# Two PSUM copies moved to ScalarE, the decay exp written into zeroed tiles, and the whole instruction order planned anew, in a fused RWKV-6 and squared-ReLU kernel

## The chip, the cores and the metric

The kernel runs on one core of a Trainium2 chip. The time is that of one whole execution in device microseconds (us). The profile of an execution has a *span*, from its first to its last instruction; the time is about 2 us longer. The *ramp* is the first 36 us, in which TensorE still waits for loads and for the other engines; behind it TensorE is saturated, which means that it has work all the time.

## The reference

```python
def _attn_ref(r, k, v, w, u):                 # (4, 8, 768, 48) each, u (8, 48)
    for t in range(S):
        cur = np.einsum('bhd,bhe->bhde', u[None] * kt, vt)
        y[:, :, t] = np.einsum('bhd,bhde->bhe', rt, state + cur)
        state = wt[:, :, :, None] * state + np.einsum('bhd,bhe->bhde', kt, vt)

def _moe_ref(x, w_in, w_out):                 # x (3072, 384), w_in (384, 2048)
    r = np.maximum(x @ w_in, 0.0)
    return (r * r) @ w_out
```

The kernel cuts the sequence into 24 chunks of 128 steps, 6 for each of 4 batch rows. In a chunk the recurrence becomes matmuls: cumulative sums of log w, decayed r and k, scores, and a state that is handed on. Two finished chunks make one of 12 blocks of the feed-forward part.

## The kernel before

Every operation is a small function, and a long list of words calls them. Each engine runs its own part of the list in order. A word in the wrong place makes an engine stand behind a wait although later work is ready.

```python
ps_cp = pool("ps_cp", bufs=1, PSUM)       # two banks: cumulative sum, its exp, scores, in turn
ps_tr_pool = pool("ps_tr", bufs=1, PSUM)  # one bank: transposes, state update, transposed y, in turn
# (pools abridged)

    other_head = consts.tile([C, HP, 2], BF16)
    nc.gpsimd.memset(other_head[:], 0.0)
    nc.gpsimd.memset(other_head[0:DP, :, 1:2], -30000.0)
    nc.gpsimd.memset(other_head[DP:C, :, 0:1], -30000.0)

    def q_(s):                                   # row sums of r*u*k
        nc.vector.reduce_sum(q[:], tiles.pop(("qp", s))[:], axis=AX.X)

    def ac_(s):                                  # decay of the state over the chunk
        a_c = tiles["a_c", s] = a_small.tile([C, HP, 2], FP32, name="a_c")
        nc.scalar.activation(a_c[:], tiles["su", s][:, DM:DM + 2 * HP]..., AF.Exp)

    def rkt_(s):                                 # transposed r and k out of PSUM
        rkT = tiles["rkT", s] = a_mid.tile([C, 2, HP, C], BF16, name="rkT")
        nc.vector.tensor_copy(rkT[:], tiles.pop(("tr", s))[:])

    def su_(s):                                  # state update
        for p in range(HP):
            nc.tensor.matmul(ps_su[:, p * 2 * D:(p + 1) * 2 * D], rdec[:, 1, 2 * p:2 * p + 2, :],
                             v_bf[:, 2 * p:2 * p + 2, :], start=True, stop=True)
        nc.tensor.matmul(ps_su[:, DM:DM + 2 * HP], ident[:], other_head[:], start=True,
                         stop=False, skip_group_check=True)
        for p in range(HP):
            nc.tensor.matmul(ps_su[:, DM + 2 * p:DM + 2 * p + 2], lw[:, 2 * p:2 * p + 2, :],
                             ones2[:], start=False, stop=True, skip_group_check=True)
    # ... (cut: all other functions)
    order = """
        ld:0:w ld:0:k warm:6:0 ld:0:u ld:0:r ld:1:w lw:0 ld:0:v cum:0 ld:1:r ub exp:0 ld:1:k ...
    """                                          # 1052 words, cut
```

`warm:n:b` is n filler matmuls on a zero tile, `ld` a load, `ld:4:I` the fifth slab of w_in (a slab is an eighth of a weight matrix; it is cast to bf16 before it is used). A tile of two heads has 128 rows; a state block is valid only where head meets head, and the mask matmul of -30000 makes exp give zero elsewhere.

Of the kernel before, what the change touches and what calls it, by code (L numbers as in the profile page):

```python
# [8 lines left out]
FP32 = mybir.dt.float32  # L9
FP16 = mybir.dt.float16  # L10
BF16 = mybir.dt.bfloat16
AF = mybir.ActivationFunctionType
# [4 lines left out]
def kernel(  # L17
# [11 lines left out]
    nc = tc.nc  # L29
# [3 lines left out]
    C = 128  # L33
    DP = 64
    HP = H // 2
    NCH = S // C
    DM = H * D
# [10 lines left out]
    consts = ctx.enter_context(tc.tile_pool(name="consts", bufs=1))  # L48
# [81 lines left out]
    ident = consts.tile([C, C], BF16)  # L130
# [6 lines left out]
    other_head = consts.tile([C, HP, 2], BF16)  # L137
    nc.gpsimd.memset(other_head[:], 0.0)
    nc.gpsimd.memset(other_head[0:DP, :, 1:2], -30000.0)
    nc.gpsimd.memset(other_head[DP:C, :, 0:1], -30000.0)  # L140
# [64 lines left out]
    def ac_(s):  # L205
        a_c = tiles["a_c", s] = a_small.tile([C, HP, 2], FP32, name="a_c")
        nc.scalar.activation(a_c[:], tiles["su", s][:, DM:DM + 2 * HP].rearrange("p (a e) -> p a e", e=2), AF.Exp)
# [14 lines left out]
    def rkt_(s):  # L222
        rkT = tiles["rkT", s] = a_mid.tile([C, 2, HP, C], BF16, name="rkT")
        nc.vector.tensor_copy(rkT[:], tiles.pop(("tr", s))[:])  # L224
# [30 lines left out]
    def su_(s):  # L255
        rdec, v_bf, lw = tiles["rdec", s], tiles["v", s], tiles["lw", s]
        ps_su = tiles["su", s] = ps_tr_pool.tile([C, 512], FP32, name="tr")
        for p in range(HP):
            nc.tensor.matmul(ps_su[:, p * 2 * D:(p + 1) * 2 * D], rdec[:, 1, 2 * p:2 * p + 2, :],  # L259
                             v_bf[:, 2 * p:2 * p + 2, :], start=True, stop=True)  # L260
        nc.tensor.matmul(ps_su[:, DM:DM + 2 * HP], ident[:], other_head[:], start=True,
                         stop=False, skip_group_check=True)
        for p in range(HP):
            nc.tensor.matmul(ps_su[:, DM + 2 * p:DM + 2 * p + 2], lw[:, 2 * p:2 * p + 2, :],  # L264
                             ones2[:], start=False, stop=True, skip_group_check=True)
# [103 lines left out]
    def ld_(n, x):  # L369
# [7 lines left out]
        ld:0:w ld:0:k warm:6:0 ld:0:u ld:0:r ld:1:w lw:0 ld:0:v cum:0 ld:1:r ub exp:0 ld:1:k warm:2:1 rd:0 lw:1 ld:2:w  # L377
        tr:0 uc cum:1 rkt:0 ld:1:v v:0 ku:0 warm:1:2 exp:1 su:0 ld:2:k warm:8:3 ac:0 rd:1 ku:1 ld:2:r lw:2 ts:0 ld:0:I
        qp:1 p:0 tr:1 pm:0 v:1 ld:2:v qp:0 warm:3:0 rkt:1 ld:3:w cum:2 sn:0 warm:1:1 exp:2 q:1 su:1 ku:2 warm:6:2 ld:3:r
        ac:1 rd:2 vq:1 ld:3:k q:0 p:1 warm:2:3 ts:1 vq:0 ld:1:I pm:1 tr:2 qp:2 y:0 lw:3 ld:4:w warm:2:0 v:2 rkt:2 cum:3  # L380
        ld:5:w warm:3:1 exp:3 ysb:0 ku:3 q:2 yt:0 y:1 ld:3:v xt:0 rd:3 warm:1:2 sn:1 su:2 ld:2:I ac:2 ysb:1 p:2
        cast:i:0:0 qp:3 warm:2:3 ts:2 ld:4:k pm:2 yt:1 vq:2 warm:2:0 xt:1 ld:3:I lw:4 tr:3 ld:4:v sn:2 q:3 m1:0:0:1 lw:5
        rkt:3 vq:3 v:3 y:2 rl:0:0 p:3 cast:i:0:1 ld:4:r su:3 pm:3 cast:i:1:0 m1:0:1:2 ku:4 ld:5:k rl:0:1 m1:0:2:3 ysb:2
        ac:3 cum:4 rw:5 ts:3 ld:5:r y:3 exp:4 cast:i:1:1 yt:2 warm:1:0 sn:3 ld:4:I ysb:3 m1:0:3:1 xt:2 v:4 yt:3 rd:4
        qp:4 ld:5:I warm:3:2 xt:3 ld:6:I rl:0:2 ld:7:I ku:5 cum:5 q:4 tr:4 ld:0:O rl:0:3 ld:1:O m1:1:0:0 gt:0:0 exp:5
        ld:2:O m1:1:2:2 kw:5 ld:3:O rkt:4 ld:5:v m1:1:3:3 rl:1:2 gt:0:1 su:4 qp:5 cast:i:2:0 m1:1:1:1 rd:5 ac:4 m1:1:4:2
        vq:4 rl:1:3 ts:4 p:4 rl:1:0 cast:i:2:1 m1:0:4:3 sn:4 rl:1:1 pm:4 ld:4:O tr:5 cast:i:3:0 ld:5:O m1:1:5:0 gt:1:1
        ld:6:w rl:0:4 m1:0:6:1 gt:1:0 rl:1:4 y:4 m1:0:5:3 rl:1:5 rkt:5 m1:1:6:2 cast:i:3:1 rl:0:5 ysb:4 rl:0:6 m1:0:7:0
        cast:o:0:1 cast:o:0:0 m1:1:7:3 gt:1:2 p:5 rl:0:7 m2:1:1:0:1 ld:6:O gt:0:2 cast:o:1:0 ld:7:O yt:4 cast:o:1:1
        m2:0:0:0:0 ld:7:w rl:1:6 q:5 m2:1:1:1:1 v:5 pm:5 vq:5 m2:0:1:0:2 cast:o:2:0 m2:0:1:1:2 ld:6:k rl:1:7 y:5  # L390
        cast:o:2:1 m2:0:0:1:0 xt:4 ysb:5 ld:6:r m2:0:0:2:0 lw:6 gt:1:3 rw:6 yt:5 cum:6 m2:1:1:2:1 xt:5 gt:0:3 cast:o:3:0
        m2:0:1:2:2 ld:7:r m1:2:0:3 exp:6 cast:o:3:1 ld:7:k m2:1:1:3:1 lw:7 m2:0:1:3:2 ku:6 rl:2:0 ld:6:v m2:0:0:3:0
        os:1:1 ld:8:w kw:6 m1:2:4:3 os:0:0 m2:1:0:0:1 ld:7:v rw:7 qp:6 rd:6 rl:2:4 m2:1:0:1:1 ld:8:k ku:7 os:0:1 q:6
        cum:7 tr:6 exp:7 ld:9:w m1:2:1:0 kw:7 rkt:6 m1:2:2:3 lw:8 ld:10:w qp:7 rd:7 m1:2:6:2 v:6 ld:9:k rl:2:2 vq:6 q:7
        tr:7 rw:8 p:6 ld:11:w rkt:7 rl:2:1 ku:8 m1:2:5:3 v:7 pm:6 ld:10:k su:6 kw:8 rl:2:5 m1:2:3:0 ld:8:r lw:10
        m2:1:0:2:1 gt:2:0 ac:6 rl:2:3 y:6 ts:6 ld:9:r p:7 lw:9 m2:1:0:3:1 sn:6 pm:7 rl:2:6 ld:8:v m2:2:1:0:3 vq:7 os:1:0
        m1:2:7:0 ysb:6 ld:11:k cum:8 gt:2:1 yt:6 y:7 exp:8 ld:10:r qp:8 m2:2:0:0:2 ysb:7 m2:2:1:1:3 ld:12:w xt:6 ku:9
        rd:8 rw:9 yt:7 m2:2:0:1:2 store:1:1 xt:7 gt:2:2 ld:9:v cum:9 kw:9 rl:2:7 tr:8 q:8 ld:12:k m1:3:2:1 exp:9 rkt:8
        vq:8 m1:3:3:0 ld:10:v rl:3:2 rd:9 qp:9 m2:2:0:2:2 v:8 m1:3:4:1 gt:2:3 rl:3:3 ld:13:w ku:10 tr:9 rl:3:4 m1:3:0:0
        ld:11:v rkt:9 rw:10 m1:3:5:1 rl:3:0 gt:3:1 ld:13:k su:7 kw:10 m2:2:0:3:2 ac:7 ld:14:k rl:3:5 ts:7 m1:3:1:0  # L400
        os:2:0 gt:3:2 ld:11:r su:8 sn:7 rl:3:1 p:8:1:2 q:9 v:10 m1:3:6:0 store:0:1 gt:3:0 lw:12 ld:12:r vq:9 m2:2:1:2:3
        pm:8 ac:8 ld:13:r rl:3:6 m2:2:1:3:3 ku:11 v:9 store:1:0 ts:8 m2:3:0:0:0 os:2:1 ld:12:v qp:10 pmh:9:0 y:8 lw:11
        m1:3:7:3 pmh:9:1 rw:12 sn:8 ld:14:r su:9 v:11 ysb:8 cum:10 m2:3:0:1:0 qp:11 ac:9 store:2:1 rl:3:7 ts:9 ld:14:w
        y:9 exp:10 q:10 yt:8 ku:12 m2:3:0:2:0 ysb:9 ld:13:v m2:3:1:0:1 xt:8 rd:10 sn:9 rw:11 yt:9 ld:15:r m2:3:1:1:1
        xt:9 q:11 kw:12 cum:12 lw:13 tr:10 exp:12 qp:12 m1:4:2:2 ld:16:r rkt:10 m1:4:0:3 gt:3:3 rl:4:2 ld:15:w su:10
        kw:11 rd:12 m1:4:3:2 ac:10 rl:4:0 store:0:0 m2:3:1:2:1 ku:13 ld:16:w ts:10 rl:4:3 cum:11 ld:14:v m1:4:4:3 gt:4:1
        exp:11 vq:10 m2:3:0:3:0 q:12 ld:15:v rl:4:4 m1:4:5:2 rd:11 qp:13 lw:14 m1:4:1:3 os:3:0 ld:15:k sn:10 q:13 tr:11
        rl:4:1 m2:3:1:3:1 rkt:11 ld:16:v rl:4:5 m1:4:6:0 gt:4:0 os:3:1 p:10:3:2 rl:4:6 store:3:1 gt:4:2 ld:16:k m1:4:7:1
        rw:14 pm:10 ld:17:w tr:12 rw:13 store:3:0 m2:4:0:0:0 kw:13 ld:17:v pmh:11:0 y:10 cum:13 pmh:11:1 vq:11
        m2:4:1:0:3 v:13 ysb:10 rl:4:7 m2:4:0:1:0 ku:14 ld:18:v rkt:12 lw:15 ld:17:r y:11 exp:13 m2:4:1:1:3 qp:14 ysb:11  # L410
        yt:10 m2:4:0:2:0 gt:4:3 xt:10 ld:17:k vq:12 m2:4:1:2:3 v:12 rd:13 ld:18:k rw:15 yt:11 kw:14 m2:4:1:3:3 xt:11
        q:14 ld:19:v cum:14 su:12 ku:16 m1:5:2:2 ac:12 exp:14 ts:12 ld:18:w m2:4:0:3:0 ku:15 tr:13 os:4:1 rd:14 m1:5:4:1
        qp:15 os:4:0 rl:5:2 rkt:13 m1:5:0:3 kw:15 rl:5:4 q:15 p:12:0:2 rl:5:0 sn:12 su:13 pm:12 m1:5:3:1 ac:13 v:14
        ku:17 m1:5:1:3 rl:5:3 ts:13 y:12 rl:5:1 cum:15 vq:14 pmh:13:0 tr:14 lw:16 m1:5:5:1 ysb:12 vq:13 lw:17 m1:5:6:3
        rkt:14 exp:15 sn:13 ld:20:v pmh:13:1 yt:12 ld:19:k m1:5:7:0 store:4:1 xt:12 gt:5:0 y:13 store:2:0 rl:5:5 su:14
        gt:5:1 ld:21:v m2:5:1:0:2 ac:14 ld:20:k v:15 ts:14 m2:5:0:0:1 rl:5:6 ysb:13 ld:19:w m2:5:1:1:2 rw:16 rd:15 yt:13
        kw:16 m2:5:0:1:1 xt:13 cum:16 rl:5:7 gt:5:2 tr:15 ld:18:r qp:16 m1:6:2:3 exp:16 rkt:15 m1:6:0:0 ld:20:w qp:17
        rl:6:2 rd:16 m2:5:1:2:2 rl:6:0 store:4:0 sn:14 su:15 q:16 m2:5:0:2:1 ac:15 v:16 gt:5:3 p:14:3:0 vq:15 lw:18
        ts:15 m2:5:0:3:1 rw:18 pm:14 sn:15 rw:17 m2:5:1:3:2 lw:19 tr:16 kw:17 pmh:15:0 os:5:1 y:14 os:5:0 cum:17
        pmh:15:1 m1:6:1:2 ku:18 v:17 store:5:0 ysb:14 m1:6:4:3 ld:19:r exp:17 kw:18 rkt:16 ld:21:w y:15 ld:22:w m1:6:3:1  # L420
        rl:6:4 rd:17 qp:18 yt:14 rl:6:1 m1:6:6:0 ysb:15 ku:19 xt:14 ld:21:k m1:6:7:3 rl:6:3 yt:15 gt:6:0 cum:18 ld:20:r
        m1:6:5:2 xt:15 vq:16 rl:6:6 m1:7:2:1 ld:21:r gt:6:1 rl:6:5 m1:7:0:0 q:17 rl:6:7 ld:22:r m1:7:3:2 gt:6:2 exp:18
# [59 lines left out]
```

## Time and profile before

| | before |
|---|---|
| time, four executions on one chip | 191.76 to 191.83, median 191.81 |
| the profiled execution: time, span | 192.89, 191.1 |
| busy: TensorE, VectorE, ScalarE, GpSimd | 97, 74, 70, 59 per cent |

The row PE of the page gives busy tenths of TensorE in 40 slices, and the row DMA the same of the 16 DMA engines. The chain follows what ended last back to what released it. The lines stand in the prediction.

### The profile page before, as it was taken

What the parts mean: (1) busy time and instruction counts of PE and PEld (TensorE: products, weight loads), DVE (VectorE), ACT (ScalarE), POOL (GpSimd) and SP (SyncE); (2) the same over time, 40 slices, a digit from 0 to 9 for tenths busy, and PEclk for the clock granted to TensorE, in tenths of its full rate; (3) what the DMA queues carried; (4) which work ended last, traced back from release to release, by engine and by line L of the source; (5) the groups of instructions that cost most, each with busy time, mean ns of one, the idle gap of its engine ahead of it and who ended that gap; (6) DMA issues with size and microseconds to landing.
All of it is one profiled execution on the core that took longest, in us unless ns stands there. A gap on an engine that the chain in (4) does not pass through costs nothing.

```text
span 191.1 us, 4952 instructions
## 1 busy us (share of the span) xinstructions
PE 184.7 (97%) x1955; PEld 137.1 (72%) x1958; DVE 140.5 (74%) x211; ACT 132.9 (70%) x284; POOL 113.2 (59%) x128
## 2 busy tenths in 40 slices
PE   6999999899999999999999999999999999999993
PEld 2444578676687787777788778777698778676873
DVE  3349999797378978799688999888787787463220
ACT  3533687887887978789589798858598468524640
POOL 7294959400985989984995897579297713000000
PEclk9999999999999999999999999999999999999998
DMA  6999999998998979999798939940620000003313
GB/s 120 204 244 244 230 215 307 372 314 229 208 196 173 234 150 234 226 219 221 171 202 171 230 105 192 192 81 3 139 71 0 0 3 0 5 0 141 110 41 124
DMA packets 107817, 30.20 MB, mean 158 GB/s; under 512 B 100498, under 2 KB 106771, under 8 KB 107795
## 3 DMA queue, kind: packets, MB, share of 16 engines
q1 hardware_dynamic: 107794, 29.89, 67.6%
q8 instruction: 15, 0.25, 0.6%
q14 instruction: 8, 0.06, 0.1%
HBM read 25.17 MB, written 4.72 MB: 156 GB/s over the span
## 4 chain that ended last, share of the span: by engine, by line
PE 80%; SPq 13%; DMA 3%; issue 1%; ACT 0%; DVE 0%
PE mm L340 32%; PE mm L316 31%; SPq L67 11%; PE tr L220 5%; DMA w_st<-in_moe_w_in_dram 3%; PE y L285 2%; PE cp L238 2%; PE tr L301 2%; PE cp L194 2%; SPq L90 2%; PE y L290 2%; PE tr L259 1%; PE mm L355 1%; PE mm L238 1%; PE tr L264 1%
## 5 line engine op out<-in xcount | busy, mean ns | idle before, releaser
L316 PE MATMUL mm<-xT,wi_sb 128*128 128x256 bf16 x576 | 72.4, 273 | 1.1 <-ACT wi_sb L105 0.8
L340 PE MATMUL mm<-wo_sb,gt 128*128 128x384 bf16 x368 | 69.2, 326 | 0.0
L325 ACT ACTIVATE rl<-mm 128x512 f16<-128x512 f32 x96 | 55.6, 599 | 14.0 <-PE mm L316 12.2
L316 PEld LDWEIGHTS <-wi_sb 128*128 128x128 bf16 x576 | 54.1, 98 | 9.7 <-ACT wi_sb L105 1.1
L340 PEld LDWEIGHTS <-gt 128*128 128x128 bf16 x368 | 34.1, 98 | 17.6
L333 DVE TENSOR_TENSOR gt<-rl 128x1024 bf16<-128x1024 f16 x48 | 36.7, 780 | 9.1 <-ACT rl L325 9.0
L176 POOL TENSOR_TENSOR ku<-rk_raw,u_bc 128x384 f32<-128x384 f32 x24 | 25.7, 1074 | 9.0 <-DMA rk_raw<-in_k_dram 5.9
L168 POOL TENSOR_TENSOR rk_raw<-rk_raw,rw 128x384 f32<-128x384 f32 x19 | 20.9, 1099 | 16.4 <-ACT rw L164 13.2
L188 POOL TENSOR_TENSOR vq<-v_raw,q 128x384 f32<-128x384 f32 x24 | 22.1, 920 | 13.9 <-DVE q L184 10.1
L211 DVE TENSOR_TENSOR rdec_buf<-rk_raw,cp 128x768 bf16<-128x768 f32 x24 | 22.8, 950 | 8.0 <-ACT cp L201 4.4
L180 POOL TENSOR_TENSOR qprod<-rk_raw,ku 128x384 f32<-128x384 f32 x24 | 25.8, 1079 | 1.6 <-issue 1.1
L224 DVE COPY rkT<-tr 128x1024 bf16<-128x1024 bf16 x24 | 16.5, 688 | 10.0 <-PE tr L220 10.0
L277 POOL TENSOR_TENSOR S<-t_state,a_c 128x384 bf16<-128x384 f32 x20 | 18.0, 900 | 7.8 <-DVE t_state L273 5.3
L243 DVE TENSOR_TENSOR pmT<-cp,tri_strict 128x1024 bf16<-128x1024 f32 x16 | 19.5, 1219 | 3.0 <-PE cp L238 3.0
L345 ACT ACTIVATE o_sb<-mm 128x384 f32<-128x384 f32 x23 | 11.1, 492 | 9.9 <-PE mm L340 9.9
L295 DVE TENSOR_TENSOR y_sb<-vq,y 128x384 bf16<-128x384 f32 x24 | 13.2, 549 | 6.1 <-PE y L290 4.3
L304 ACT COPY xT<-tr 128x384 bf16<-128x384 bf16 x24 | 11.5, 481 | 7.3 <-PE tr L301 7.1
L367 PE MATMUL mm<-warm 128*128 128x512 bf16 x40 | 14.2, 474 | 1.4 <-DVE warm L133 1.3
L220 PE MATMUL tr<-ident,rdec_buf 128*128 128x128 bf16 x192 | 15.1, 223 | 0.1
L220 PEld LDWEIGHTS <-rdec_buf 128*128 128x128 bf16 x192 | 12.9, 100 | 3.1 <-issue 1.0
L160 ACT ACTIVATE lw_buf<-w_raw 128x384 bf16<-128x384 f32 x24 | 12.3, 522 | 3.1 <-POOL lw_buf L146 1.8
L184 DVE TENSOR_REDUCE q<-qprod 128x8 f32<-128x384 f32 x24 | 13.1, 545 | 0.1
(59 smaller groups left out, 197.2 us busy)
## 6 DMA issues: line engine op xcount, KB each, us to landing
w_raw<-in_w_dram SPq DMA_DIRECT2D x24, 192.0 KB, 3.8
rk_raw<-in_k_dram SPq DMA_DIRECT2D x24, 192.0 KB, 3.9
rk_raw<-in_r_dram SPq DMA_DIRECT2D x24, 192.0 KB, 3.7
v_raw<-in_v_dram SPq DMA_DIRECT2D x24, 192.0 KB, 4.0
out_dram<-o_sb SPq DMA_DIRECT2D x23, 192.0 KB, 3.1
w_st<-in_moe_w_in_dram SPq DMA_DIRECT2D x8, 384.0 KB, 5.7
w_st<-in_moe_w_out_dram SPq DMA_DIRECT2D x8, 384.0 KB, 7.1
out_dram<-o_sb SPq DMA_DIRECT2D x2, 96.0 KB, 1.6
```

The source lines that it names most:

```text
L67: nc.sync.dma_start(out=dst, in_=src[b, :, c * C:(c + 1) * C, :].rearrange("h c d -> c h d"))
L168: nc.gpsimd.tensor_mul(k_s, k_s, tiles.pop(("rw", s))[:])
L176: nc.gpsimd.tensor_mul(ku[:], raw["rk", s][:, 1], u_bc[:])
L180: nc.gpsimd.tensor_mul(qp[:], raw["rk", s][:, 0], tiles.pop(("ku", s))[:])
L188: nc.gpsimd.tensor_mul(vq[:], raw["v", s][:], tiles.pop(("q", s))[:, :, None].to_broadcast([C, H, D]))
L211: nc.vector.tensor_mul(rdec[:, :, :, 0:D], raw["rk", s][:], tiles.pop(("cs", s))[:, :, 0:DM].rearrange("p a (h d) -> p a h d", h=H))
L220: nc.tensor.transpose(ps_tr[:, i, p, :], rdec[:, i, 2 * p:2 * p + 2, :], ident[:])
L243: nc.vector.tensor_mul(pmT[:].rearrange("p e a t -> p (e a) t"), tiles.pop(("p", s))[:].rearrange("p e (a t) -> p (e a) t", a=HP), tri_str ...
L316: nc.tensor.matmul(ps1[:, j * width:(j + 1) * width], wi_sb[:, kk, n * 128:(n + 1) * 128], xT[:, kk, s0 * C:s0 * C + width], start=(kk == ...
L325: nc.scalar.activation(tiles["rl", i, q][:, j], tiles.pop(("m1", i, g))[:], AF.Relu, scale=RS)
L333: nc.vector.tensor_mul(tiles["gt", i][:, 4 * q:4 * q + 4, :].rearrange("p a b -> p (a b)"), rl, rl)
L340: nc.tensor.matmul(tiles["m2", i, mt][:, 0:DM], gt[:, n, mt * 128:(mt + 1) * 128], wo_sb[:, n, :], start=(n == 0), stop=(n == NT - 1))
```

## The change

It takes the mask matmul away: the decay exp writes the two valid halves into tiles that were zeroed once. It lets ScalarE copy transposed r and k out of PSUM for chunks 2 and 3. And it orders the whole list anew.

```diff
-    other_head = consts.tile([C, HP, 2], BF16)
-    ... three memsets
+    NAC = 3
+    ac_bufs = []
+    for i in range(NAC):
+        t = consts.tile([C, HP, 2], FP32, name=f"ac_buf{i}")
+        nc.gpsimd.memset(t[:], 0.0)
+        ac_bufs.append(t)
@@ ac_
-        a_c = tiles["a_c", s] = a_small.tile([C, HP, 2], FP32, name="a_c")
-        nc.scalar.activation(a_c[:], tiles["su", s][:, DM:DM + 2 * HP]..., AF.Exp)
+        a_c = tiles["a_c", s] = ac_bufs[s % NAC]
+        for e in range(2):
+            rows = slice(e * DP, (e + 1) * DP)
+            nc.scalar.activation(a_c[rows, :, e], tiles["su", s][rows, DM:DM + HP], AF.Exp)
@@ rkt_
-        nc.vector.tensor_copy(rkT[:], tiles.pop(("tr", s))[:])
+        copy = nc.scalar.copy if s in (2, 3) else nc.vector.tensor_copy
+        copy(rkT[:], tiles.pop(("tr", s))[:])
@@ su_
-        nc.tensor.matmul(ps_su[:, DM:DM + 2 * HP], ident[:], other_head[:], start=True, ...)
         for p in range(HP):
-            nc.tensor.matmul(ps_su[:, DM + 2 * p:DM + 2 * p + 2], lw[:, 2 * p:2 * p + 2, :],
-                             ones2[:], start=False, stop=True, skip_group_check=True)
+            nc.tensor.matmul(ps_su[:, DM + p:DM + p + 1], lw[:, 2 * p:2 * p + 2, :],
+                             ones2[:, 0:1], start=True, stop=True, skip_group_check=True)
@@ order (1052 words become 1051; two excerpts, cut)
-  ... ld:2:k ... ld:2:r ... ld:0:I ld:2:v ... ld:3:w ld:3:r ld:3:k ld:1:I ld:4:w ld:5:w ...
+  ... ld:2:k ld:2:w ld:2:r ld:3:w ld:2:v ld:3:k ld:3:r ld:4:w ld:0:I ld:3:v ld:1:I ld:2:I ...
-  VectorE around chunk 9: ... rd:9 gt:2:3 rkt:9 gt:3:1 ts:7 gt:3:2 q:9 ...
+  VectorE around chunk 9: ... rd:9 q:9 gt:3:1 rkt:9 gt:3:2 ts:7 ...
```

## The prediction

> **What bounds the kernel now.** I read the page's busy shares first, then its chain, then the tensor engine's timeline in the two places where the change touches it, then the chain around the last place where that engine stood still. First the page:
>
> ```profile
> PE 184.7 (97%) x1955; PEld 137.1 (72%) x1958; DVE 140.5 (74%) x211; ACT 132.9 (70%) x284; POOL 113.2 (59%) x128
> PE   6999999899999999999999999999999999999993
> DMA  6999999998998979999798939940620000003313
> PE 80%; SPq 13%; DMA 3%; issue 1%; ACT 0%; DVE 0%
> ```
>
> TensorE is busy almost throughout. That alone proves little: part of it is filler (matmuls on a zero tile that only keep the clock up), and modelled matmul ends overlap. So I use starts. The chain has two parts: DMA up to about 34 us, then TensorE without a break. This is where they meet:
>
> ```profile
> 27.00 6.63 DMA w_st<-in_moe_w_in_dram
> 33.63 0.02 issue
> 33.65 0.89 ACT wi_sb L105
> 34.54 0.05 issue
> 34.59 0.83 PE mm L316 x6
> ```
>
> The fifth slab of the first weight matrix lands at 33.65, ScalarE casts it in 0.89, and the first matmul that reads it starts at 34.59. The waits of TensorE from 34.6 us to the end name only this one:
>
> ```profile
> PE mm L316 <- ACT wi_sb L105: 0.8, 1, 0.8
> ```
>
> The timeline there:
>
> ```profile
> 32.63 0.33 PE L259 MATMUL tr<-v_bf,rdec_buf 128*128 128x96 bf16 x4
> 32.80 0.17 PE L261 MATMUL tr<-other_head,ident 128*128 128x8 bf16 x1
> 32.83 0.24 PE L264 MATMUL tr<-ones,lw_buf 128*128 128x2 bf16 x4
> 32.93 0.81 PE L316 MATMUL mm<-xT,wi_sb 128*128 128x256 bf16 x6
> 34.59 0.83 PE L316 MATMUL mm<-xT,wi_sb 128*128 128x256 bf16 x6 [0.84 <-ACT wi_sb L105]
> 35.35 0.40 PE L238 MATMUL cp<-rkT 64*128 64x128 bf16 x8
> 35.68 0.83 PE L316 MATMUL mm<-xT,wi_sb 128*128 128x256 bf16 x6
> ```
>
> The end:
>
> ```profile
> 185.42 2.65 PE mm L355 x32
> 188.07 0.02 issue
> 188.10 0.36 DVE o_sb L360
> ```
>
> So the span of 191.1 is 34.59 until the slab is usable, 188.07 - 34.59 = 153.48 of TensorE, and 3.03 for the last eviction and store.
>
> Is there slack within the 153.48? I count the work left at 34.59 with spacings from the timeline. 528 first-layer matmuls at 0.109 (twelve in 1.31) are 57.6; 368 of the second at 0.163 (four in 0.65) are 59.8; the last 32 take 2.65; 152 transposes at 0.0556 take 8.5; 60 transposes of y at 0.054 take 3.2; y takes 160 at 0.025 and 68 at 0.042, 6.9; 18 cumulative sums at 0.165 take 3.0; the score matmuls 5.7 (4 singles at 0.33, 8 pairs at 0.55); 15 state updates at 0.30 take 4.5. The sum is 151.9. A group of six after score matmuls takes 0.76 instead of 0.655, so twelve switches add about 1.2: 153.1. Slack is about 0.4 us: a new order cannot win much there, only lose.
>
> **What the Trainium skill says.** "TensorE: Matmul & The Clock Gate", section "Wait — 56ns, not 53.3ns?", gives N/2.4 GHz plus about 2.5 ns from start to start when warm, and a floor of about 25 ns however small N is. The trace agrees: eight transposes in 0.45, four 2-column matmuls in 0.10. So halving the columns of those four from 2 to 1 saves nothing; only the removed instruction counts.
>
> "ScalarE: Activation LUTs", section "What ACT_TABLE_LOAD costs", gives 186 ns plus 0.833 ns per element for an ACTIVATE with immediate operands, and an overlap of about 93 ns back to back. This trace has 178 for 8 elements and 599 for 512, so it agrees.
>
> "Perfetto Trace Analysis", section "Identifying the Most-Contended Engine", is the reason why I counted starts: the skill warns against matmul busy time. The trace agrees: the four tiny matmuls show 163 ns each and occupy 25.
>
> **The change part by part.**
>
> One: the 8-column matmul of the identity with the -30000 mask goes, in 20 state updates. From its start to the next start is 0.03 (32.80 to 32.83). Five of the 20 lie before the wait at 33.65, which swallows them. The other 15 lie on the saturated part: 15 x 0.03 = 0.45 us off the end.
>
> Two: the decay exp becomes two activations on 64 partitions x 4 elements, where one on 128 x 8 took 178 ns. By the page's overlap each extra one adds 178 - 93 = about 85 ns to ScalarE: 20 x 0.085 = 1.7 us over an engine 70% busy. Off the path, as long as relu evictions still come in time. GpSimd keeps three tiny memsets ahead of the work, before the first zeroed decay buffer now; the first logarithm started at 3.82, long after that buffer's memset at 1.78 to 2.31, so the start does not move.
>
> Three: two copies of 128x1024 go from VectorE (688 ns) to ScalarE. By the page 186 + 0.833 x 1024 = 1039 ns, an estimate; this trace supports the slope. VectorE loses 1.4 us, ScalarE gains 2.1. This copy lies on the ramp's own chain. There, one two-bank PSUM buffer serves in turn the cumulative sum, its exp, and the scores: chunk 2's sum starts at 14.83, chunk 3's at 19.31, chunk 4's at 27.07. In it VectorE is the queue: scores done near 17.6, but masking waits until 18.03 for two reductions. With the copies away and the reductions moved, masking chunk 1 can begin about 17.65. Following the new order by hand with the durations above, I get chunk 3's sum near 18.9, the first weight matmul near 23.2 instead of 24.0, chunk 4's sum near 26.4 instead of 27.07, and the eighth weight matmul group finished near 32.7 instead of 33.58. These are estimates: about 0.8 us sooner at the doorstep of the slab.
>
> Four: the loads. The new order fetches r, k, v, w of chunks 2 and 3 before slab 0. But up to slab 4 both orders issue the same 28 transfers: w, k, r of chunks 0 to 5, v of 0 to 4, u, and slabs 0 to 3. At most eight are in flight (each issue waits for the eighth before it), and the DMA row is 9 nearly throughout those slices. A reordering of the same bytes through a full pipe lands slab 4 at the same time, 33.6, give or take 0.4. TensorE arrives sooner and idles longer.
>
> What is put into that idle time counts. The old order has the scores of chunk 4 after the wait (0.33, 35.35 to 35.68) and a 0.76 group behind it. The new order has them before it, ready near 33.0 and done by 33.3. That takes 0.33 plus the 0.10 switch, 0.43 us, out of the saturated part.
>
> Five: the rest of the order. Behind the slab I followed the new words to the second layer: slab 5 is needed near 35.9 and its cast on VectorE, queued behind the state addition, should end near 35.8; slab 6 near 36.6 for 36.9; scores of chunk 5 near 38.9 for 38.9. Narrow but enough. Later the relu buffers, decay buffers and output buffers have the same counts; I expect no gain and a small risk. One more output store is held back to the end; at the 0.5 us that a store moves in (the profile moves 192 KB at about 360 GB/s) it should be through before the last eviction. I give it nothing.
>
> Sum: 0.45 + 0.43 = 0.88, from 191.8 to 190.9 us.
>
> **The rivals.**
>
> The ramp is a chain of dependences, not DMA: then the 0.8 us of part three comes through to the end (with 0.45 on top, 190.5), and slab 4 would have to land earlier. For it: TensorE has filler all through the ramp, so it waits for others there. Against it: the fifth slab is what ended the last wait, and ScalarE itself was idle 0.88 before its cast.
>
> The new order stalls: a slab's cast or a relu comes late, as ScalarE carries 3.8 us more and the two-part decay exp stands before a state addition that waits for it (VectorE waited 3.1 us for that exp in the kernel before, off the path). For it: margins of 0.0 to 0.3 in part five. Against it: before had no such wait in 153 us, with ScalarE at 70%. It would cost 0.3 to 1.5: 191.2 to 192.4.
>
> The slab lands at another time because the mix in flight differs: plus or minus 0.4.
>
> The ScalarE copy is slower than VectorE's by 0.35, twice, on the ramp's chain: it eats part of the 0.8, and the slab hides it. No effect on the end.
>
> **Range and chances.** The 0.45 is nearly sure. The 0.43 depends on the slab's landing and on the casts behind it. Landing 0.4 sooner and the remaining 0.4 slack found gives 190.0; gains lost to one stall of 1 us gives 192. So 190.0 to 192.0 holds it 8 times in 10. Two per cent is 3.8 us, more than all idle time that is left to win; slower by as much needs a chain of stalls. I give 0.02 faster, 0.96 same, 0.02 slower.
>
> **What would show it.** The line of the mask matmul is gone, and 15 state updates after the ramp are 0.03 shorter each. The fifth slab's cast by ScalarE again starts near 33.6, its idle time longer than 0.88. TensorE's last real wait lies before that cast and is longer than 0.84, 1.0 to 1.5. The scores of chunk 4 stand before it. From there to the last matmul 152.6 instead of 153.48. I am wrong if the slab lands more than 0.5 from 33.65, if the first wait is no longer for it, or if TensorE waits again after it for 0.3 us or more.

## The result, and the profile after

Four executions of the changed kernel took 191.94 to 192.69 us, median 192.38, beside 191.81 of the kernel before. A ratio in this text is the mean time of one kernel's fast runs over that of the other's of the same rounds, so it is not quite the ratio of the medians. Here it is 1.0028, with an interval of 1.0007 to 1.0049. By the rule of 2 per cent that is the same. But the time lies above the predicted range of 190.0 to 192.0.

The profile says something else than the time. It was taken in the execution of 192.52. Its span is 190.3, where the prediction worked out to 191.1 - 0.88 = 190.2. The page of the changed kernel:

```profile
PE 182.4 (96%) x1936; PEld 136.0 (71%) x1936; DVE 140.7 (74%) x209; ACT 139.8 (73%) x306; POOL 113.6 (60%) x128
PEclk9789999999999999999999999999999999999999
PE 75%; DMA 6%; POOL 6%; ACT 4%; DVE 3%; issue 3%; SPq 2%; DVEq 0%; POOLq 0%; ACTq 0%
```

ScalarE has 6.9 us more, where I had worked out 3.8. The chain no longer splits into DMA and TensorE alone: GpSimd, ScalarE and VectorE now stand in it.

The start of the saturated part. The cast of the fifth slab, in the timeline of ScalarE:

```profile
32.16 0.90 ACT L105 CAST wi_sb<-w_st 128x768 bf16<-128x768 f32 x1 [0.63 <-DMA w_st<-in_moe_w_in_dram]
```

And what TensorE does around it, in its own timeline:

```profile
31.81 0.82 PE L319 MATMUL mm<-xT,wi_sb 128*128 128x256 bf16 x6
32.46 0.38 PE L370 MATMUL mm<-warm 128*128 128x512 bf16 x1
32.95 0.40 PE L243 MATMUL cp<-rkT 64*128 64x128 bf16 x8
33.28 2.16 PE L319 MATMUL mm<-xT,wi_sb 128*128 128x256 bf16 x18
```

The fifth slab is cast at 32.16 instead of 33.65, and TensorE does not wait for it: it goes from the scores of chunk 4 straight into that slab's matmuls at 33.28. Then come waits that the kernel before did not have. TensorE's waits of the changed kernel from 30 us on:

```profile
PE tr L264 <- DVE rkT L229: 0.5, 1, 0.5
PE tr L304 <- DVE y_sb L298: 0.2, 1, 0.2
```

The first is at 68.8 us. The chain in that stretch shows what stood behind it (columns: start, length, what):

```profile
61.83 1.36 POOL vq L190
63.19 1.40 POOL rk_raw L170
...
65.52 1.01 POOL qprod L182
66.52 0.02 issue
66.55 0.09 DVE q L186
66.63 0.38 issue
67.02 1.12 DVE gt L336
68.14 0.61 DVE rkT L229
68.75 0.04 issue
68.79 0.33 PE tr L264 x4
```

VectorE takes its words in order. The new order puts the row sum of chunk 9 (q) ahead of the copy of its transposed r and k (rkT). The row sum waits for GpSimd's product, and GpSimd was still busy. So the copy is late, though it needs nothing from GpSimd, and TensorE needs the PSUM bank that the copy frees. Loads stand behind GpSimd: of the four profiles of the changed kernel, three had waits of TensorE at 68 to 70 us, and in these GpSimd stood 1.0 to 1.7 us for loads of r between 36 and 70 us; in the fourth, without waits, it stood 0.3. The two go together; that the one causes the other is not shown, since no run held the loads back on purpose.

Where TensorE's time went can be added up. For every group of matmuls I take the start of the next group, less its own start, less its count times the usual spacing (0.109 us for 256 columns, 0.1625 for 384, 0.216 for 512, 0.0556 for a transpose, 0.025 to 0.042 for the short ones). What is left is lost. Fillers are not work, so in the first 36 us they are added to it. Below zero means that my spacings are a little too long; only differences count. A group that begins before a boundary counts wholly before it.

| profile | first 36 us | 36 to 80 us | 80 to 190 us | span | time less span |
|---|---|---|---|---|---|
| before, three profiles | 18.6, 18.8, 18.2 | -0.5, -0.5, -0.6 | -1.3, -1.3, -1.5 | 191.1, 191.5, 190.9 | 1.8, 1.8, 1.8 |
| changed, four profiles | 16.9, 17.6, 16.9, 17.5 | 1.0, -0.4, 1.1, 2.5 | -1.8, -1.5, -1.9, -1.8 | 190.3, 189.5, 190.2, 192.1 | 2.2, 2.2, 2.2, 2.3 |
| new operations in the old order, three profiles | 17.9, 17.1, 17.9 | -0.4, -0.3, -0.4 | -1.3, -1.4, -1.3 | 190.3, 189.6, 190.4 | 1.8, 1.8, 1.8 |

The mean of the changed kernel against that of before: 1.3 gained in the ramp, 1.6 lost between 36 and 80 us, 0.4 gained behind, and 0.5 for the removed matmuls (20 at 0.026, measured below). That is 0.6 less, and the spans differ by 0.6. The last column then takes 0.4 of it away. That column hardly varies: 2.17 to 2.29 in all 22 executions of the changed kernel for which there is a span, 1.72 to 1.86 in those of the kernel before. The ramp column has a rival that no run tested, the clock; see what stays open.

### The profile page after: what moved, and what is told of

The parts are those of the page before. It is cut to its first block, busy times and chain, and to the rows that moved or that the text cites. A ratio compares the mean times of both kernels' runs of the same rounds, so it can differ in the third digit from the quotient of the medians.

```text
span 190.3 us, 4953 instructions
## 1 busy us (share of the span) xinstructions
PE 182.4 (96%) x1936; PEld 136.0 (71%) x1936; DVE 140.7 (74%) x209; ACT 139.8 (73%) x306; POOL 113.6 (60%) x128
## 4 chain that ended last, share of the span: by engine, by line
PE 75%; DMA 6%; POOL 6%; ACT 4%; DVE 3%; issue 3%; SPq 2%; DVEq 0%; POOLq 0%; ACTq 0%
PE mm L319 27%; PE mm L343 25%; PE tr L224 5%; PE mm L370 3%; DMA rk_raw<-in_r_dram 2%; PE y L288 2%; PE tr L304 2%; POOL qprod L182 2%; DMA rk_raw<-in_k_dram 2%; DMA w_raw<-in_w_dram 2%; PE cp L243 2%; PE tr L264 2%; POOL rk_raw L170 2%; PE cp L196 2%; PE y L293 1%
## 5 line engine op out<-in xcount | busy, mean ns | idle before, releaser
L319 PE MATMUL mm<-xT,wi_sb 128*128 128x256 bf16 x576 | 74.2, 272 | 0.0
L343 PE MATMUL mm<-wo_sb,gt 128*128 128x384 bf16 x368 | 70.0, 326 | 0.0
L328 ACT ACTIVATE rl<-mm 128x512 f16<-128x512 f32 x96 | 55.5, 598 | 14.7 <-PE mm L319 12.6
L343 PEld LDWEIGHTS <-gt 128*128 128x128 bf16 x368 | 34.6, 98 | 17.8
L336 DVE TENSOR_TENSOR gt<-rl 128x1024 bf16<-128x1024 f16 x48 | 38.4, 807 | 9.3 <-ACT rl L328 9.3
L178 POOL TENSOR_TENSOR ku<-rk_raw,u_bc 128x384 f32<-128x384 f32 x24 | 24.8, 1036 | 7.8 <-DMA rk_raw<-in_k_dram 5.3
L182 POOL TENSOR_TENSOR qprod<-rk_raw,ku 128x384 f32<-128x384 f32 x24 | 26.7, 1119 | 3.5 <-DMA rk_raw<-in_r_dram 1.8
L280 POOL TENSOR_TENSOR S<-t_state,ac_buf 128x384 bf16<-128x384 f32 x20 | 18.8, 940 | 16.1 <-DVE t_state L276 13.4
L229 DVE COPY rkT<-tr 128x1024 bf16<-128x1024 bf16 x22 | 15.1, 686 | 6.2 <-PE tr L224 5.4
L370 PE MATMUL mm<-warm 128*128 128x512 bf16 x41 | 13.5, 447 | 1.3 <-DVE warm L133 1.3
## 6 DMA issues: line engine op xcount, KB each, us to landing
w_raw<-in_w_dram SPq DMA_DIRECT2D x24, 192.0 KB, 4.1
rk_raw<-in_k_dram SPq DMA_DIRECT2D x24, 192.0 KB, 3.8
rk_raw<-in_r_dram SPq DMA_DIRECT2D x24, 192.0 KB, 3.8
v_raw<-in_v_dram SPq DMA_DIRECT2D x24, 192.0 KB, 3.7
out_dram<-o_sb SPq DMA_DIRECT2D x23, 192.0 KB, 2.7
```

Source lines behind the costliest of these rows:

```text
L178: nc.gpsimd.tensor_mul(ku[:], raw["rk", s][:, 1], u_bc[:])
L182: nc.gpsimd.tensor_mul(qp[:], raw["rk", s][:, 0], tiles.pop(("ku", s))[:])
L319: nc.tensor.matmul(ps1[:, j * width:(j + 1) * width], wi_sb[:, kk, n * 128:(n + 1) * 128], xT[:, kk, s0 * C:s0 * C + width], start=(kk == ...
L328: nc.scalar.activation(tiles["rl", i, q][:, j], tiles.pop(("m1", i, g))[:], AF.Relu, scale=RS)
L336: nc.vector.tensor_mul(tiles["gt", i][:, 4 * q:4 * q + 4, :].rearrange("p a b -> p (a b)"), rl, rl)
L343: nc.tensor.matmul(tiles["m2", i, mt][:, 0:DM], gt[:, n, mt * 128:(mt + 1) * 128], wo_sb[:, n, :], start=(n == 0), stop=(n == NT - 1))
```

## The experiments

The times of one kernel turned out to differ from execution to execution and from chip to chip, so each set has the kernel before beside it. Runs 1 to 4 were on chip B, 5 to 8 on C, 9 to 12 on D, 13 to 16 on E, 17 and 18 on F. These are all timed sets of the kernels that answer the main question. Ratio: fast runs only, with its interval. Means: of all runs, because the cut for fast runs (1.5 per cent over the fastest) removes four of the eleven times of the kernel before on chip B, and none of the changed kernel.

| set | kernel before, mean (range) | this kernel, mean | ratio |
|---|---|---|---|
| first chip, changed | 191.81 (191.76 to 191.83) | 192.35 | 1.0028 (1.0007 to 1.0049) |
| chip B, changed | 192.86 (190.87 to 194.59) | 192.29 | 1.0016 (0.9961 to 1.0072) |
| chip D, changed | 193.01 (192.55 to 194.05) | 192.48 | 0.9973 (0.9939 to 1.0006) |
| chip F, changed | 193.99 (192.65 to 195.74) | 194.08 | 1.0014 (0.9983 to 1.0046) |
| chip B, new operations, old order | 192.86 | 192.53 | 1.0023 (0.9970 to 1.0075) |
| chip E, new operations, old order | 192.41 (190.97 to 193.72) | 191.79 | 0.9960 (0.9921 to 0.9999) |
| chip F, new operations, old order | 193.99 | 192.59 | 0.9940 (0.9906 to 0.9974) |

My theory after the first result was: the operations help as predicted, and the new order loses it again. Rivals: the operations do not help (ScalarE's extra work hurts), or chance.

**1. The kernel before again**, unchanged.

> The kernel before, unchanged, as a control. The record has two things that do not fit: the changed kernel's profiled span is 0.8 us shorter (190.3 against 191.1), its time 0.57 us longer (192.38 against 191.81). Theory A, the first profile of before was a slow draw: this copy's span is near 189.5 and time minus span near 2.25, as in the four runs of the changed kernel. Theory B, something outside the span grew with the change: this copy's span is again near 191.1 and time minus span near 0.7 to 1.8. In both its ratio to before is 1.000.

192.25 to 193.55, ratio 1.0048 (1.0003 to 1.0093), span 191.5, time less span 1.79. The kernel is the same, so on this chip the ratio of fast runs can be off by as much as that: four long times of the set beside it are cut as slow, and none of these six. The means of all times are 193.03 and 192.86. Neither theory holds whole: the span is long again, but time less span is the same 1.8 as in the first profile. What was odd was the set of four times within 0.07 us. On this chip the eleven other times of the same kernel went from 190.87 to 194.59.

**2. The changed kernel again.**

> The changed kernel, unchanged, for more runs. It ran 191.94 to 192.69 in four runs where before kept within 0.07. Theory A (the gain is lost to waits of TensorE inside the span): ratio again 1.001 to 1.005, and the spread of 0.3 us or more stays. Theory B (chance of one chip): ratio 0.995 to 1.000.

191.69 to 193.67, ratio 1.0016 with an interval from 0.9961: unclear. Span 189.5, with no wait of TensorE of 0.2 us or more after 36 us. So the waits at 61 to 78 us come in some executions and not in others. A run that lacks them in its one profile therefore proves little, which bears on runs 6 and 8.

**3. New operations, old order.**

> All changes of operations (mask matmul gone, two-part decay exp into zeroed tiles, two copies on ScalarE) with the order of before. If the operations do what the prediction says, 0.3 to 0.5 us faster than before (ratio 0.9975 to 0.9985) and no new wait of TensorE behind the slab. If the second activation and the ScalarE copies hurt, ratio over 1.001.

Ratio 1.0023, interval 0.9970 to 1.0075: undecided, and repeated below. The span was 190.3, against 191.5 of the kernel before in the same set.

**4. Old operations, new order.**

> The new order alone on the operations of before. If the order brings the loss (waits of TensorE at 68 and 77 us and an unsteady ramp), this is 0.5 to 1.2 us slower than before (ratio 1.003 to 1.006). If the order is neutral, ratio 0.998 to 1.001.

Ratio 1.0063 (1.0012 to 1.0114), span 192.4. Waits behind the ramp: 0.7 for the decay multiply, 0.7 for a y addition and 0.4 for a copy. The times do not show that the order alone is slower, since the control in run 1 read 1.0048; by the means of all times it is 193.31 beside 192.86. The profile, of the slowest of the six executions, does show the loss: between 36 and 80 us, worked out as above, 2.1, where the kernel before has -0.5.

**5. One store moved back.**

```diff
- ... os:11:0 store:11:0 store:10:1 store:9:0 last:11:1:0:0 last:11:1:1:1
+ ... store:9:0 m2:10:0:3:2 ... os:11:0 store:11:0 store:10:1 last:11:1:0:0 last:11:1:1:1
```

> The changed kernel with one word of its order moved: the held-back output store (block 9, first half) is issued before the second layer of block 10 ends instead of last but two. In five profiled runs of the changed kernel time minus span was 2.22 to 2.29, in two of the kernel before 1.79, with the old order on the new operations 1.82, with the new order on the old operations 2.08. Theory A (that store lengthens the end outside the span): time minus span falls to 1.8. Theory B (it is something else in the order): it stays at 2.1 to 2.3.

192.79 - 190.6 = 2.19. That store is not what lengthens the time outside the span. Ratio 0.9988, nothing gained. The only wait of TensorE from 36 us on was one of 0.2, at 68 us.

**6. Row sums behind the copies.** The store as in 5, and:

```diff
- ... q:8 ... ysb:7 ... rd:8 ...      rd:9 q:9 gt:3:1 rkt:9 ...      ku:12 ... vq:9 ...
+ ... ysb:7 ... rd:8 q:8 ...          rd:9 gt:3:1 rkt:9 q:9 ...      vq:9 ku:12 ...
```

> As the run before, and the row sums of chunks 8 and 9 on VectorE moved behind the decay multiply of chunk 8 and the copy of transposed r and k of chunk 9, and the product of chunk 9 on GpSimd moved ahead of the u-times-k product of chunk 12. Theory A (TensorE's waits at 61, 68 and 77 us in the changed kernel come from VectorE standing behind GpSimd, which stands behind late loads): those three waits are gone and the span is near 189.0 to 189.5, time 190.9 to 191.6. Theory B (loads late by themselves, the order of the engines' queues does not matter): waits of the same sum appear elsewhere, time 192.

The waits at 61, 68 and 77 us are not in its profile, and TensorE's waits from 36 us on are these:

```profile
PE cp L196 <- DVE pmT L248: 0.3, 1, 0.3
PE mm L319 <- DVE pmT L256: 0.2, 1, 0.2
PE cp L243 <- DVE rkT L229: 0.2, 1, 0.2
```

Ratio 1.0002: nothing gained, as theory B had it. Whether the move took the three waits away is not shown: run 5, without the move, had only one of 0.2 left, and run 2 none. What the chain above shows is that TensorE stood behind the row sum of chunk 9 in that execution. The row sums are not the whole cause, because VectorE is late around 70 us with them moved too.

**7 and 8. Fewer loads.** Chunk 0's w for all chunks, in both kernels; wrong results (relative error 0.14).

```diff
+        if part == "w" and step > 0:
+            raw["w", step] = raw["w", 0]
+        elif part in "wv":
```

> The kernel before, but all chunks take w of chunk 0, so 23 of 24 loads of w (4.5 of 25.2 MB read) are gone; wrong result on purpose. Theory A (loads set the ramp and make the runs of one kernel differ by 1 to 3 us): the slab arrives earlier, the time falls by 1 us or more, and the runs lie within 0.6 us of each other. Theory B (the ramp is a chain of dependences and the spread is something else, such as the phase of TensorE's clock): time falls by under 0.5 us and the spread stays at 1 us or more.

> The changed kernel with the same loads taken away; wrong result on purpose. If loads were behind the waits of TensorE at 61 to 77 us, they are gone here, and its span is 0.4 to 0.9 us below that of the kernel before with the same loads away (mask matmul 0.45, and up to 0.4 from the ramp). If the new order is itself slower, its span is equal or longer.

The old order gained: mean 191.75 beside 192.62, ratio 0.9950 (0.9910 to 0.9991), four of six times within 0.05. For the new order no gain is shown: 190.37 to 193.62, mean 192.55, ratio 0.9944 with an interval that reaches 1.0005. Its profile has no wait at 60 to 78 us, which fits that late loads have a part in those, but run 2 had none with all loads. Its ramp lost as much as with all loads, and its times were spread wider than those of the changed kernel in any set. So in the one profile of each, loads bound part of the old ramp, as I had read it, but not the new one, and they do not explain the spread. Its time less span was only 1.80 to 1.92, with the order of the changed kernel to the end.

**9. New order on the engines, old order of loads.** One load was hoisted, because it was needed earlier.

> The changed kernel with the order of loads and stores of the kernel before on the DMA queue (one load hoisted, because it is needed earlier), and its own order on the five engines. Theory A (the new order of loads made the slab land sooner, but chunk 8 to 12 late): the fifth slab is cast by ScalarE at 32.8 us or later, and the waits of TensorE at 50 to 78 us shrink to under 0.5 in sum. Theory B (the engines' order does both): slab cast at 31.6 to 32.2 and waits at 60 to 78 us stay at 0.4 to 1.0. Time minus span: 1.8 if the DMA queue's order sets it, 2.2 if the engines' order does.

205.21, ratio 1.0628: 12 us slower. TensorE's four longest waits from 36 us on:

```profile
PE cp L243 <- DVE rdec_buf L215: 3.0, 2, 2.6
PE tr L224 <- DVE t_state L276: 2.5, 1, 2.5
PE tr L264 <- DVE t_state L276: 1.3, 1, 1.3
PE tr L304 <- DVE t_state L276: 1.1, 1, 1.1
```

Theory A failed. The order of loads and that of the engines are one plan; this half of it alone is worse than none. The slab's cast came at 34.43. As a way of telling the two apart this run was of little use, and it shows how little slack the loads have.

**10. Old order on the engines, new order of loads.**

> The mirror image: changed operations, order of before on the five engines, order of loads and stores of the changed kernel (one load hoisted). Theory A: ramp as good as in the changed kernel, and TensorE waits at 50 to 78 us; time minus span 2.2 if the DMA queue's order sets it. Theory B: no such waits, time minus span 1.8.

191.85 to 195.30, median 192.43, ratio 0.9956 from the fast runs; the profile fell in a slow one (195.29, span 193.5), so its waits are not compared with those of fast runs. Time less span is 1.79. With 9 (2.05) this says: what sits outside the span goes more with the engines' order than with the DMA queue's. In this slow profile TensorE stood 2.0 us for one of the copies on ScalarE, up to 26.4 us, and the granted clock was 0.5 from 27.6 to 31.0; twelve matmuls of 256 columns took 2.27 us from 27.06 on, where 1.31 is usual.

**11. The mask matmul nine times**, same result.

```diff
+        for _ in range(9):
             nc.tensor.matmul(ps_su[:, DM:DM + 2 * HP], ident[:], other_head[:], start=True, ...)
```

> The kernel before with its 8-column mask matmul issued nine times in each state update instead of once, same result. By the prediction each costs 0.03 us, so the 15 state updates on the saturated part grow by 15 x 8 x 0.03 = 3.6 us, 4.8 with all 20 (the skill's floor of 25 ns gives 3.0 and 4.0). Rival: short matmuls hide behind weight loads or other work, under 1 us in all.

Ratio 1.0197 (1.0166 to 1.0227), 3.8 us by the means. In the timeline of TensorE:

```profile
34.77 0.33 PE L259 MATMUL tr<-v_bf,rdec_buf 128*128 128x96 bf16 x4
34.94 0.37 PE L262 MATMUL tr<-other_head,ident 128*128 128x8 bf16 x9
35.17 0.24 PE L265 MATMUL tr<-ones,lw_buf 128*128 128x2 bf16 x4
```

Nine take 35.17 - 34.94 = 0.23, so one takes 0.026. All 20 x 8 added ones are 4.1 us, those of the 15 updates behind the ramp 3.1; the time grew by 3.8. The price of the part removed is settled, and the rival that they are hidden falls.

**12. The changed kernel, third profile.**

> The changed kernel again, for another profile and more times. If its waits at 60 to 78 us are a matter of chance of when loads land, they again differ from the two profiles so far (1.0 and none). Ratio to before 0.997 to 1.003 if the two are equal.

Ratio 0.9973, and waits of TensorE of 0.4, 0.2 and 0.2 us behind 36 us. The forecast of chance held.

**13 and 14. Where the time outside the span comes from.** The last 100 words, or the first 150, taken from the old order.

```diff
- (last 100 words of the new order)         - (first 150 words of the new order)
+ (last 100 words of the old order)         + (first 150 words of the old order)
```

> The changed kernel, with its last 100 words of the order taken from the order of before (same work, on the engines and the DMA queue). Time minus span is 1.77 to 1.83 in all seven profiles with the old order on the engines, and 1.88 to 2.29 in all ten with the new one. Theory A (the end of the program sets it): here 1.8. Theory B (the start or the middle): here 2.1 to 2.3.

> The changed kernel, with its first 150 words taken from the order of before. Theory A (the end sets time minus span): 2.1 to 2.3. Theory B (the start): 1.8. No forecast for the span: the two orders are not fitted to each other at the seam, waits of some us are likely.

(Counted again, six profiles with the old order on the engines and eight with the new one were there by then.) Old tail: 193.9 - 192.1 = 1.8. Old head: 192.47 - 190.0 = 2.5. So the last 100 words have a part in the 0.4 us that the time has and the span has not. They are not the whole: run 8 ends with the same words as the changed kernel and has 1.80 to 1.92 in its six executions. The old tail's span is long because the two orders do not fit at the seam: TensorE lost 1.6 us there, at 156 to 160 us. Each was run once.

**15. New operations, old order, second set.**

> Changed operations with the order of before, again, since one set of six times on one chip could not tell 0.3 us from nothing. If the removed mask matmul gives its 0.45 to 0.6 us: 0.3 to 0.6 below the runs of before of the same rounds (ratio 0.997 to 0.9985). If the two extra ScalarE loads eat it: 0.999 or more.

Ratio 0.9960 (0.9921 to 0.9999), 0.6 us by the means: the upper end of the forecast.

**16. The kernel before, third profile.**

> The kernel before again, for a third profile: what does a typical execution look like? The first profile (span 191.1, time 192.89) was 1.1 us slower than the four times beside it (191.76 to 191.83). If that one was an untypical draw, the wait for the fifth slab (0.84 us of TensorE at 33.7 us) is shorter or absent here, as it was in the second profile (0.2); if it is typical, 0.6 to 1.0.

The wait for the slabs that ScalarE casts was 1.2 us in all, so of the three profiles it was 0.8, 0.2 (of the weight loads alone) and 1.2. The first profile was not odd in this. It was the four times beside it that were short: 44 times in other sets on four chips have means of 192.41 to 193.01.

**17 and 18. Both versions on one chip.**

> The changed kernel against the kernel before once more, on whatever chip comes. Means of all runs so far: chip of the first runs +0.5 us, and -0.57 and -0.53 us on two other chips where the kernel before spread over 1.5 to 3.7 us. Theory A (the true difference is the 0.88 us of the prediction less the 0.43 us that the end of the new order adds outside the span): mean 0.2 to 0.8 below before. Theory B (no gain, the first comparison is right): 0.0 to 0.6 above.

> Changed operations with the old order, beside the changed kernel on one chip. It has the removed matmuls and the old end (time minus span 1.8), but not the new ramp. So far 0.33 and 0.63 us below before. If it is the best of the three: mean 0.3 to 0.8 below before, and equal to or below the changed kernel.

The changed kernel: ratio 1.0014 (0.9983 to 1.0046), 0.1 us above by the means, as theory B had it. The new operations in the old order: 0.9940 (0.9906 to 0.9974), 1.4 us below, more than forecast. TensorE's waits from 36 us on, first of the changed kernel, then of the new operations in the old order:

```profile
PE cp L196 <- DVE rdec_buf L215: 0.8, 1, 0.8
PE tr L304 <- ACT cp L206: 0.6, 1, 0.6
PE tr L264 <- DVE rkT L229: 0.5, 1, 0.5
PE tr L304 <- DVE y_sb L298: 0.2, 1, 0.2
```

```profile
PE cp L196 <- DVE rdec_buf L215: 0.3, 1, 0.3
```

The version with the new operations and the old order had the lowest mean of the three on this chip, and on the other two chips it was below the kernel before by the means. On chip B the ratio of the fast runs is 1.0023, undecided; there the changed kernel's mean was the lowest. So against the kernel before it gained 0.3 to 1.4 us by the means. Against the changed kernel two chips have both, and they differ: 0.2 us slower on B, 1.5 us faster on F.

## Why the prediction was wrong, point by point

**The class was right and the time was not.** "Same" held in three of the four sets of the changed kernel, and the one on chip B came out unclear. The time of 192.38 lies 0.4 over the range.

**The step that failed first: the base.** "0.45 + 0.43 = 0.88, from 191.8 to 190.9" takes a saving read from one profile, whose execution took 192.89, off the median of others that took 191.8. If those executions had the same work and were 1.1 us shorter, they had lost 1.1 us less somewhere. On other chips the same kernel had means of 192.4 to 194.0. Against its own execution the prediction would have read 192.89 - 0.88 = 192.0. The range of 1 us either way was also too narrow for a kernel whose eleven times on one chip can cover 3.7 us; four times within 0.07 hid that.

**The step that failed most: "I expect no gain and a small risk" of the order behind the ramp.** The second rival, that the new order stalls, is what happened, but mostly by another way than I gave. I had a slab's cast or a relu of ScalarE come late. ScalarE ended one wait each in two of the four profiles (a relu 0.4 us, an exp 0.6); the others were ended by VectorE, which in the chain shown stood behind GpSimd, and GpSimd goes with the loads. The prediction gave a figure for this stretch: from the slab's first matmul to the last matmul 152.6 us. The first profile has 187.27 - 33.28 = 153.99, and the other three have 152.65, 154.65 and 155.65. The 152.65 is of the profile without waits: the count of the work was right, and what it left out are the waits. The mean loss between 36 and 80 us was 1.6 us more than before, and it varied from none to 3 us. The sign was in the profile before: the row DMA has 9 in 18 of the 25 slices up to 120 us. I read "DMA up to about 34 us, then TensorE" from the chain, because in that one execution nothing came late.

**A term that was missing: time outside the span.** It is 1.8 us in every profile with the old order on the engines and 2.2 in the changed kernel, 0.4 us. One store is cleared, and the last 100 words have a part (runs 5, 13 and 14); run 8 shows that they do not do it alone. The traces have a candidate that I did not look at: in all eleven profiles with the new order on the engines, a packet of 8 KB of the kind "instruction" starts after the span, 0.6 us after it in the two profiles with 1.8 to 1.9 outside, about 1.0 in the seven with 2.2 to 2.5, and 1.7 in the two with 2.0 to 2.1. The nine with the old order have none. It does not rise in step, so it stays a candidate, and the cause stays open.

**Part one, the mask matmul: right, a little too large.** I had 0.03 each and 0.45; nine in a row give 0.026, so 0.39 on the 15 updates. The ramp did not swallow the other five for certain, since TensorE does not wait for the slab in the changed kernel.

**Part two, the second exp: right about the path, wrong in size.** The view of the tile:

```profile
L211 ACT ACTIVATE ac_buf<-tr x40: 152/169/176, 11.6 to 161.8; 64x4 f32<-64x4 f32 x40
```

The two halves start 0.18 apart in the chain (20.33 and 20.51), so they do not overlap by 93 ns and each costs its full 0.17. ScalarE gained 6.9 us and not 3.8: 40 at 0.169 in place of 20 at 0.178 are 3.2, the copies 2.0, and the rest is not accounted for. In the old order the same ScalarE work cost TensorE one wait of 0.3 behind 36 us, for the decay multiply; two of the three profiles of before have the same wait at 0.2.

**Part three, the copies: right.** They took 1012 ns, estimated 1039. (What stood before masking chunk 1 was one row sum and one state addition, not two reductions.) The hand-drawn ramp gave the first weight matmul near 23.2 and the eighth group finished near 32.7; it was 22.72 and 32.46.

**Part four, the slab: wrong, and for a reason that I had called a rival.** Its cast began at 31.2 to 32.2 in the four profiles of the changed kernel, at 32.4 to 33.7 in three of before and 32.2 to 32.9 with the new operations in the old order. "The same bytes through a full pipe land at the same time" is too strong, even by the kernel before alone, where it moved by 1.3 us. Two things moved. The slab was issued at 26.2 to 27.0 us in the changed kernel and at 27.0 to 28.3 in before; and from issue to landing it took 4.9 to 5.4 us against 5.4 to 6.6. The 6.63 that the prediction was read from is the longest of the ten profiles of the table. (The new order also loads v of chunk 3 behind slab 0 and not before it.) So the first rival came true as well: the new ramp is not bound by that slab. By the table it saves 1.3 us and not 0.43. That gain, larger than mine, and the loss behind it, which I left out, nearly cancel; this is why the profiled span came out at 190.3 beside my 190.2. That was luck and not a confirmation.

**What stays open.** Whether the copies on ScalarE or chance gave the new operations in the old order 0.9 us in the ramp: no run had the copies alone. Why the times are spread so differently from chip to chip. TensorE's clock may have a part: in the ramp of the changed kernel the granted clock was 0.74 from 5 to 10 us, and 0.68 from 20 to 25 us in the second profile of the kernel before, just after TensorE had stood 2.0 us for a decay multiply. The first full clock came at 12.6, 4.7 and 9.3 us in the three profiles of before, and at 4.0, 10.7, 5.1 and 10.5 in the four of the changed kernel, so a part of the 1.3 us of the ramp may be the clock's. No run tested it.

## What to carry to other kernels

Take a saving off the time of the execution that it was read from, and before trusting a range look at more than one set of runs. When one engine is saturated and its wait list is empty in a profile, this does not say that there is slack behind it: look whether loads are still full in the same stretch, and ask of every in-order queue what its next word waits for. Work added to the saturated engine cost its counted price, and taking it away is read as the same; a new global order paid in one stretch and cost in another. And where a wait comes in some executions only, one profile without it does not show that an edit removed it.

## What the Trainium skill lacked or had wrong

- "ScalarE: Activation LUTs", section "What ACT_TABLE_LOAD costs": back-to-back activations are said to overlap by about 93 ns. The two halves of one exp started 0.17 to 0.18 us apart at a length of 0.17, so there was no overlap; two relus of 0.60 in a row took 1.08, so these did overlap. The length formula is 13 to 27 ns too long: 1012 ns measured for 1024 elements, 1039 by the page.
- "TensorE: Matmul & The Clock Gate", section "Wait — 56ns, not 53.3ns?": the page's example for the floor of about 25 ns is N = 32; here it was 26 ns for 8 columns with a weight load each.
- The same page, section "Seeing it yourself", warns of clock records. Here the page of the kernel before shows a granted clock of 1.00 from 5 to 15 us although eight 512-column fillers took 3.16 us from 9.94 on, and at the warm spacing eight take 1.7; the record has no entry before the first change, at 12.6 us. Spacing is the safer sign.
- No page tells that the time of an execution exceeds its profile's span by an amount that differs with the order of the program: 1.8 us in the kernel before, 2.2 in the changed one.
- No page tells how much one kernel's times differ: four within 0.07 us on one chip, eleven over 3.7 us on another.
